# Blockwise causal attention and a gated MLP on one core: Q of the later batches loaded in 2 KB runs, transposed by the crossbar, and read by the score matmuls with a stride

## The chip, the core and the metric

The kernel runs on one core of one Trainium2 chip. The metric is device time in microseconds, the median of several runs. Most executions of one kernel agree within a little over 1%, so differences of a few us are only read from runs of the same rounds, made on the same chip.

## The reference, cut to what matters

```python
# q, k, v: [8 batches, 8 heads, 576 tokens, 64], float32
scores = q @ k.T / 8                         # per batch and head
scores = where(query_token // 64 >= key_token // 64, scores, -1e9)
attn   = softmax(scores)                     # rows
x      = (attn @ v), heads side by side      # [4608, 512]
h      = x @ w_in                            # [512, 2048]
g      = h * sigmoid(beta * h)
out    = g @ w_out                           # [4608, 512], float32
```

## The kernel before

A small planner takes operations with estimated durations, priorities and buffers, simulates them, and writes from that a fixed order of instructions for each engine. The engines then run their orders with semaphore waits only. So an estimate given to the planner changes nothing in an instruction, but it changes the order.

Work goes by head pairs: four per batch, 32 in all. For each pair, K and Q must lie transposed ([128 = 2 heads x 64, tokens]), bfloat16. In batches 0 and 1 TensorE transposes them. In batches 2 to 7 they are loaded as rows of tokens, cast by GpSimd (POOL) and transposed by the DMA crossbar. Both loads of a pair share these parts:

```python
# batches 2..7, every second pair: one load for two pairs, five DMAs, runs of 64 floats = 256 bytes
z = [g.dma_start(ST[ts.slot][:, i, :, :], src[b, h, 128*i:128*i+128, :].rearrange("h p d -> p h d"))
     for i in range(4)]
z.append(g.dma_start(ST[ts.slot][0:64, 4, :, :], src[b, h, 512:576, :].rearrange("h p d -> p h d")))
ld[nm, u] = ld[nm, u + 1] = P.op("SP", 5 * 400, fl, deps=szero, tiles=[ts], xfer=3200, prio=u, ...)
# cast on POOL
o = P.op("POOL", 740, fn, deps=[ld[nm, u]], tiles=[ts, tn], prio=u)
# crossbar transpose, issued from SP: [128 tokens x 5, 128] -> [128, 640]; 1000 and 1500 are planner estimates
g.dma_start_transpose(dst[td.slot][:].rearrange("c (t n) -> c t n", n=128), nat[tn.slot][:, 0:640])
cps[nm] = P.op("SP", 1000, ft, deps=[o], tiles=[td, tn], xfer=1500, prio=-1, ...)
...
# scores^T of a pair: K is stationary, Q streams; the two heads use rows 0-63 and 64-127 of the array
for t, q0, q1, off in blocks:
    for h in range(2):
        r = slice(64 * h, 64 * h + 64)
        z = g.matmul(o, KT[tk.slot][r, 128*t:128*t+m], QT[tq.slot][r, q0:q1])
...
# after attention: TensorE transposes the output, VectorE copies it to xT
return g.tensor_copy(xT[:, c, S*b:S*(b+1)], PSb[:, px.slot, 0:576])
```

The blocks of a pair are 512, 448, 64, 64, 320 and 192 query columns. Two groups of instructions recur in the trace: "x8" (512 + 448 + 64 + 64 columns, two heads each) and "x4" (320 + 192). ACT exponentiates the scores, POOL zeroes the masked parts of E, and TensorE multiplies by V. The MLP then works on chunks of 512 tokens (64 matmuls by `w_in`, 64 by `w_out`), and it fills TensorE between the pairs. All loads, transposes and stores are issued from one in-order queue, SP.

The softmax here doesn't subtract the row's maximum and nothing guards it: scores larger than these inputs give would overflow.

Of the kernel before, what the change touches and what calls it, by code (L numbers as in the profile page):

```python
# [7 lines left out]
bf16 = mybir.dt.bfloat16  # L8
# [262 lines left out]
def bass_blockwise_causal_attn__then__act_swish_beta_kernel(  # L271
# [10 lines left out]
    with es:  # L282
        def sb(name, shape, dt):
            return es.enter_context(nc.sbuf_tensor(name, shape, dt))

        NQ = 2
        NE = 3
        NS = 5
        ST = [sb(f"ST{i}", [128, 5, 4, 64], f32) for i in range(NS)]
        ST6 = [s[0:96].rearrange("p t h d -> p (t h d)")[:, 0:768].rearrange("p (h j d) -> p h j d", h=2, j=6)  # L290
               for s in ST]
        Vs = [sb(f"Vs{i}", [128, 5, 8, 64], f32) for i in range(NQ)]
        Qn = [sb(f"Qn{i}", [128, 768], bf16) for i in range(NQ)]
        Kn = [sb(f"Kn{i}", [128, 768], bf16) for i in range(NQ)]
        Vn = [sb(f"Vn{i}", [128, 5, 8, 66], bf16) for i in range(NQ)]
        QT = [sb(f"QT{i}", [128, 640], bf16) for i in range(3)]
        KT = [sb(f"KT{i}", [128, 640], bf16) for i in range(3)]
# [18 lines left out]
        P = Plan()  # L316
# [18 lines left out]
        def mk(fn):  # L335
            return lambda g, e: fn(g)
# [10 lines left out]
        ones, vzero = [], []  # L347
        for i in range(NQ):
            o = P.op("DVE", 300, mk(lambda g, i=i: g.memset(Vs[i][:, 4, :, :], 0.0)), prio=-8)
            vzero.append(o)  # L350
            o = P.op("POOL", 200, mk(lambda g, i=i: g.memset(Vn[i][:, 4, :, 64:66], 0.0)), prio=-5)
            ones.append(o)
            ones.append(P.op("POOL", 200, mk(lambda g, i=i: g.memset(Vn[i][:, 0:4, :, 64:65], 1.0)), prio=-5))
            for h in range(2):
# [7 lines left out]
                  xfer=100, dma=("d_beta", 1), prio=0.1)  # L362
# [3 lines left out]
                  deps=[bt, c2], tiles=[tb], lat=400, mode="full", prio=5)  # L366
# [3 lines left out]
        szero = [P.op("DVE", 350, mk(lambda g, i=i: g.memset(ST[i][64:128, 4, :, :], 0.0)), prio=-7)  # L370
                 for i in range(NS)]


        win, wout = [], []
        for a in range(4):
# [11 lines left out]
        load, ld = {}, {}  # L387
        tl = {}
        for b in range(B):
            ts, t = P.tile("Vs"), P.tile("V")  # L390
            tl[b] = t
            for h0, h1 in ([(0, 2), (2, 8)] if b == 0 else [(0, 8)]):
                def fv(g, e, ts=ts, b=b, h0=h0, h1=h1):
                    z = []
                    for i in range(4):
                        z.append(g.dma_start(  # L396
                            Vs[ts.slot][:, i, h0:h1, :],
                            v[b, h0:h1, 128 * i:128 * i + 128, :].rearrange("h p d -> p h d")))
                    for o in range(2):
                        z.append(g.dma_start(  # L400
                            Vs[ts.slot][64 * o:64 * o + 64, 4, h0 + o:h1:2, :],
                            v[b, h0 + o:h1:2, 512:576, :].rearrange("h p d -> p h d")))
                    return z

                n = (h1 - h0) / 8
                o = ld["V", b, h0] = P.op("SP", 6 * 400, fv, deps=vzero, tiles=[ts], xfer=5000 * n,
                         prio=(0.5 if h0 == 0 else 2.5) if b == 0 else 4 * b + 0.5 - 3 * (b > 1), dma=["d_V", h0, 6])

                def fw(g, e, ts=ts, t=t, h0=h0, h1=h1):
                    return g.tensor_copy(Vn[t.slot][:, :, h0:h1, 0:64], Vs[ts.slot][:, :, h0:h1, :])  # L410

                o = P.op("POOL", 300 + 2140 * n, fw, deps=[o, *ones], tiles=[ts, t],
                         prio=4 * b + (0.5 if h0 == 0 else 1))
                for h in range(h0, h1, 2):
                    load[4 * b + h // 2] = o
# [4 lines left out]
        for u in range(NU):  # L420
            b, c = divmod(u, NPAIR)
            Tv = tl[b]
            tq, tk = P.tile("QT"), P.tile("KT")
            cps = {}
            for nm, td, src, nat, dst in (("Q", tq, q, Qn, QT), ("K", tk, k, Kn, KT)):
                tn = P.tile(nm)
                if b < 2:

                    ts, pt = P.tile("ST"), P.tile("P1")

                    def fl(g, e, ts=ts, src=src, b=b, c=c):
                        return [g.dma_start(ST6[ts.slot].rearrange("p h j d -> p h (j d)"),
                                            src[b, 2 * c:2 * c + 2].rearrange("h (p j) d -> p h (j d)", j=6))]

                    o = ld[nm, u] = P.op("SP", 420, fl, tiles=[ts], xfer=1050, prio=u, dma=["d_S", 0, 1])

                    def fn(g, e, ts=ts, tn=tn, nat=nat):
                        return g.tensor_copy(nat[tn.slot][0:96, :].rearrange("p (j h d) -> p j h d", j=6, h=2),
                                             ST6[ts.slot].rearrange("p h j d -> p j h d"))

                    o = P.op("DVE", 470, fn, deps=[o], tiles=[ts, tn], prio=-1)

                    def ft(g, e, tn=tn, pt=pt, nat=nat):
                        for i in range(6):
                            z = g.transpose(PSb[:, pt.slot, 96 * i:96 * i + 96],
                                            nat[tn.slot][0:96, 128 * i:128 * i + 128], identB[0:96, 0:96])
                        return z

                    o = P.op("PE", 6 * 57, ft, deps=[o, c4], tiles=[tn, pt, td], lat=6 * 57 + 170, mode="full",
                             prio=pr(u))  # L450

                    def fc(g, e, pt=pt, td=td, dst=dst):
                        return g.tensor_copy(dst[td.slot][:, 0:576].rearrange("c (p j) -> c p j", j=6),
                                             PSb[:, pt.slot, 0:576].rearrange("c (j p) -> c p j", j=6))

                    cps[nm] = P.op("DVE", dve_t(576), fc, deps=[o], tiles=[pt, td], prio=0)
                    continue

                if c % 2 == 0:
                    ts = stage[nm] = P.tile("ST")  # L460

                    def fl(g, e, ts=ts, src=src, b=b, c=c):
                        h = slice(2 * c, 2 * c + 4)
                        z = [g.dma_start(ST[ts.slot][:, i, :, :],  # L464
                                         src[b, h, 128 * i:128 * i + 128, :].rearrange("h p d -> p h d"))
                             for i in range(4)]
                        z.append(g.dma_start(ST[ts.slot][0:64, 4, :, :],
                                             src[b, h, 512:576, :].rearrange("h p d -> p h d")))
                        return z

                    ld[nm, u] = ld[nm, u + 1] = P.op("SP", 5 * 400, fl, deps=szero, tiles=[ts], xfer=3200, prio=u,
                                                     dma=["d_S5", 0, 5])
                ts = stage[nm]

                def fn(g, e, ts=ts, tn=tn, nat=nat, c=c):
                    a = 2 * (c % 2)
                    return g.tensor_copy(nat[tn.slot][:, 0:640].rearrange("p (t h d) -> p t h d", t=5, h=2),  # L477
                                         ST[ts.slot][:, :, a:a + 2, :])

                o = P.op("POOL", 740, fn, deps=[ld[nm, u]], tiles=[ts, tn], prio=u)  # L480

                def ft(g, e, tn=tn, td=td, nat=nat, dst=dst):
                    return [g.dma_start_transpose(dst[td.slot][:].rearrange("c (t n) -> c t n", n=128),
                                                  nat[tn.slot][:, 0:640])]

                cps[nm] = P.op("SP", 1000, ft, deps=[o], tiles=[td, tn], xfer=1500, prio=-1, dma=["d_T" + nm, 0, 1])
            te = P.tile("E")
            ex = []
            zs = []
            for g0 in range(4):  # L490
                ps = P.tile("PP" if g0 < 3 else "P1")

                def fq(g, e, ps=ps, g0=g0, tq=tq, tk=tk):
                    blocks = {0: [(0, 0, 512, 0)], 1: [(1, 128, 576, 0), (0, 512, 576, 448)],
                              2: [(2, 256, 576, 0), (3, 384, 576, 320)], 3: [(4, 512, 576, 0)]}[g0]
                    for t, q0, q1, off in blocks:
                        m = min(128, 576 - 128 * t)
                        for h in range(2):
                            r = slice(64 * h, 64 * h + 64)
                            if g0 < 3:  # L500
                                o = PS[0:m, ps.slot + h, off:off + q1 - q0]
                            else:
                                o = PS[r, ps.slot, 0:64]
                            z = g.matmul(o, KT[tk.slot][r, 128 * t:128 * t + m], QT[tq.slot][r, q0:q1])  # L504
                    return z

                o = P.op("PE", 220 if g0 < 3 else 60, fq, deps=[cps["Q"], cps["K"]], tiles=[ps, tq, tk, te],
# [209 lines left out]
```

## Time and profile before

| | before |
|---|---|
| time, median of 3 | 389.35 us (388.67 to 390.41) |
| span of the profiled run | 389.1 us |
| TensorE busy / not busy | 349.6 / 39.5 us |
| SP's DMA packets | 135,744 |

These are lines of the page: engine busy times, then, in 40 slices of the span, the granted TensorE clock and the DMA busy share in tenths.

```profile
PE 349.6 (90%) x2709; PEld 176.3 (45%) x2753; DVE 168.4 (43%) x347; ACT 209.4 (54%) x306; POOL 96.6 (25%) x204
...
PEclk9985779999999569999999999999999999999999
DMA  7989979897998799698967798413001102002002
```

The reader should see the two dents in the clock row. The first, after slice 3, is the start-up. The second, in slices 14 and 15 (about 126 to 146 us), belongs to the stall that the prediction dissects.

### The profile page before, as it was taken

The numbers are of one execution on the slowest core, as the hardware profiler recorded it, in microseconds if no ns is written. First come the engines' busy times: TensorE is split into PE (matmuls) and PEld (weight loads), VectorE is DVE, ScalarE is ACT, GpSimd is POOL, SyncE is SP. The second block draws the span as 40 slices with busy tenths as digits, with TensorE's granted clock in tenths as the row PEclk, the third lists the DMA queues.
The fourth block names the chain that finished last, engine by engine and source line by source line (L and its number), as shares of the span: only waits on it lengthen the run. The fifth ranks groups of instructions, "written<-read, shape, count | busy, mean of one in ns | idle before, by whom it ended". The sixth has DMA issues, their size and how long they took to land.

```text
span 389.1 us, 6936 instructions
## 1 busy us (share of the span) xinstructions
PE 349.6 (90%) x2709; PEld 176.3 (45%) x2753; DVE 168.4 (43%) x347; ACT 209.4 (54%) x306; POOL 96.6 (25%) x204
## 2 busy tenths in 40 slices
PE   3875969999895789999999999999999999999986
PEld 1552435444452445445545555454554444444432
DVE  5753585217520437413752266512670460550710
ACT  3641648127813458456883788817861551751721
POOL 4390263432202522244153353401100000000000
PEclk9985779999999569999999999999999999999999
DMA  7989979897998799698967798413001102002002
GB/s 173 194 113 229 225 123 180 182 211 168 240 199 176 186 178 199 135 184 205 189 144 167 185 170 144 91 54 89 2 1 56 54 1 83 27 0 83 27 27 81
DMA packets 140384, 50.27 MB, mean 129 GB/s; under 512 B 128560, under 2 KB 135744, under 8 KB 140352
## 3 DMA queue, kind: packets, MB, share of 16 engines
q1 hardware_dynamic: 135744, 45.64, 54.1%
q0 software_dynamic: 4608, 4.20, 7.3%
q8 instruction: 21, 0.34, 0.4%
q14 instruction: 11, 0.09, 0.1%
HBM read 36.71 MB, written 9.44 MB: 119 GB/s over the span
## 4 chain that ended last, share of the span: by engine, by line
PE 68%; DMA 8%; SPq 8%; ACT 7%; DVE 6%; issue 2%; POOL 0%
PE PS L603 29%; PE PS L627 28%; PE PS L546 5%; ACT E L511 5%; PE PS L504 4%; SPq L396 3%; DMA ST<-in_q_dram 3%; ACT th L611 2%; DVE gT L615 2%; DMA KT<-Kn 2%; PE PS L573 2%; SPq L464 2%; DMA w_in<-in_moe_w_in_dram 1%; SPq L400 1%; DMA out_dram<-ost 1%
## 5 line engine op out<-in xcount | busy, mean ns | idle before, releaser
L603 PE MATMUL PS<-xT,w_in 128*128 128x512 bf16 x550 | 135.3, 394 | 6.6 <-DVE xT L579 2.7
L615 DVE SCALAR_TENSOR_TENSOR gT<-th,PS 128x512 bf16<-128x512 f32 x144 | 97.5, 685 | 91.2 <-ACT th L611 91.0
L627 PE MATMUL PS<-w_out,gT 128*128 128x512 bf16 x558 | 125.1, 379 | 4.4 <-DVE gT L615 2.2
L611 ACT ACTIVATE th<-PS,beta 128x512 f32<-128x512 f32 x144 | 98.0, 698 | 42.3 <-PE PS L603 41.1
L511 ACT ACTIVATE E<-PS 128x1024 bf16<-128x1024 f32 x96 | 94.6, 1035 | 40.1 <-PE PS L504 39.9
L627 PEld LDWEIGHTS PS<-w_out,gT 128*128 128x128 bf16 x576 | 54.9, 98 | 68.4 <-DVE gT L615 3.4
L603 PEld LDWEIGHTS PS<-xT,w_in 128*128 128x128 bf16 x576 | 54.0, 101 | 68.9 <-issue 7.8
L638 ACT ACTIVATE ost<-PS 128x512 f32<-128x512 f32 x33 | 19.7, 597 | 94.0 <-PE PS L627 92.2
L504 PE MATMUL PS<-QT,KT 64*128 64x448 bf16 (+5 forms) x384 | 40.9, 303 | 6.6 <-ACT E L511 3.1
L546 PE MATMUL PS<-Vn,E 128*128 128x65 bf16 x960 | 38.0, 201 | 5.5 <-POOL E L519 3.5
L546 PEld LDWEIGHTS PS<-Vn,E 128*128 128x128 bf16 x960 | 35.3, 102 | 12.7 <-POOL E L519 6.6
L579 DVE COPY xT<-PS 128x576 bf16<-128x576 bf16 x32 | 14.5, 454 | 44.1 <-PE PS L573 44.1
L556 DVE RECIPROCAL inv<-PS 128x5 f32<-128x5 f32 x64 | 8.3, 173 | 55.5 <-PE PS L546 55.1
L517 POOL MEMSET E<- 64x128 bf16 x64 | 13.6, 212 | 64.8 <-ACT E L511 60.7
L504 PEld LDWEIGHTS PS<-QT,KT 64*128 64x128 bf16 (+1 forms) x384 | 14.8, 99 | 31.4 <-issue 10.5
L564 DVE TENSOR_TENSOR xq<-PS,inv 128x320 bf16<-128x320 f32 x64 | 28.5, 486 | 0.0
L410 POOL CAST Vn<-Vs 128x2560 bf16<-128x2560 f32 (+2 forms) x9 | 18.8, 2085 | 24.0 <-DMA Vs<-in_v_dram 22.1
L477 POOL CAST Qn<-ST 128x640 bf16<-128x640 f32 x24 | 17.3, 722 | 29.4 <-DMA QT<-Qn 26.7
L477 POOL CAST Kn<-ST 128x640 bf16<-128x640 f32 x24 | 17.3, 723 | 22.0 <-DMA KT<-Kn 19.4
L519 POOL MEMSET E<- 64x256 bf16 x32 | 10.1, 316 | 43.0 <-ACT E L511 42.5
L573 PE MATMUL PS<-identB,xq 128*128 128x128 bf16 (+1 forms) x160 | 17.5, 224 | 1.5 <-DVE xq L564 1.4
L573 PEld LDWEIGHTS PS<-identB,xq 128*128 128x128 bf16 (+1 forms) x160 | 12.5, 100 | 11.8 <-DVE xq L564 2.1
(31 smaller groups left out, 71.3 us busy)
## 6 DMA issues: line engine op xcount, KB each, us to landing
out_dram<-ost SPq DMA_DIRECT2D x36, 256.0 KB, 2.3
Vs<-in_v_dram SPq DMA_DIRECT2D x28, 256.0 KB, 4.6
ST<-in_q_dram SPq DMA_DIRECT2D x48, 128.0 KB, 2.8
ST<-in_k_dram SPq DMA_DIRECT2D x48, 128.0 KB, 2.7
ST<-in_q_dram SPq DMA_DIRECT2D x8, 288.0 KB, 4.2
ST<-in_k_dram SPq DMA_DIRECT2D x8, 288.0 KB, 4.4
w_in<-in_moe_w_in_dram POOLq DMA_DIRECT2D x16, 128.0 KB, 5.7
w_out<-in_moe_w_out_dram POOLq DMA_DIRECT2D x16, 128.0 KB, 4.3
```

Source lines behind the costliest of these rows:

```text
L410: return g.tensor_copy(Vn[t.slot][:, :, h0:h1, 0:64], Vs[ts.slot][:, :, h0:h1, :])
L477: return g.tensor_copy(nat[tn.slot][:, 0:640].rearrange("p (t h d) -> p t h d", t=5, h=2), ST[ts.slot][:, :, a:a + 2, :])
L504: z = g.matmul(o, KT[tk.slot][r, 128 * t:128 * t + m], QT[tq.slot][r, q0:q1])
L511: return g.activation(E3[te.slot][:, g0, :, :], PS[:, ps.slot:ps.slot + 2, :], ACT.Exp, scale=0.125)
L546: z = g.matmul(o, eblk(te, t, i, h), Vn[Tv.slot][:, t, 2 * c + h, 0:65], start=(t == 0), stop=(t == i))
L564: return g.tensor_tensor(xq[tx.slot][:, :, 64 * w:64 * w + 64], a, x, ALU.mult)
L573: z = g.transpose(PSb[:, px.slot, 128 * i:128 * i + r], xq[tx.slot][0:r, i, :], identB[0:r, 0:r])
L603: z = g.matmul(PS[:, ph.slot, :], w_in[:, c, 128 * j:128 * j + 128], xT[:, c, row:row + RC], start=(c == 0), stop=(c == 3))
L611: return g.activation(th[tt.slot][:], PS[:, ph.slot, :], ACT.Tanh, scale=beta[:, j:j + 1])
L615: return g.scalar_tensor_tensor(out=gT[tg.slot][:, j, :], in0=th[tt.slot][:], scalar=1.0, in1=PS[:, ph.slot, :], op0=ALU.add, op1=ALU.mult)
L627: z = g.matmul(PS[:, po.slot, :], gT[tg.slot][:, j, 128 * w:128 * w + 128], w_out[:, j, :], start=(j == 0), stop=(j == NJ - 1))
L638: return g.activation(ost[to.slot][:], PS[:, po.slot, :], ACT.Copy, scale=0.5)
```

## The change

The intent: fewer, longer DMA packets and fewer issues for Q, to relieve SP and the DMA engines. Each partition takes 8 consecutive tokens of two heads, so that a run is 8 x 64 floats = 2 KB. After the cast (72 partitions x 1024) the crossbar gives `QT[c, j*80 + p]` for token `8p + j`. The score matmuls then take the tokens in order by stepping 80 elements (160 bytes) between neighbours. K can't be treated alike without also permuting V. At the same time, estimates of the planner are replaced by values meant to be closer to the measured ones: V issue and transfer, K issue, transpose issue and transfer. In the planner a transfer lands 0.7 us + its entered time + 1.5 us after its issue begins, and the entered times of all DMAs are booked one after another.

```diff
--- before.py
+++ after.py
@@ -289,8 +289,10 @@
         ST = [sb(f"ST{i}", [128, 5, 4, 64], f32) for i in range(NS)]
         ST6 = [s[0:96].rearrange("p t h d -> p (t h d)")[:, 0:768].rearrange("p (h j d) -> p h j d", h=2, j=6)
                for s in ST]
+        ST8 = [s[0:72].rearrange("p t h d -> p (t h d)")[:, 0:1024].rearrange("p (h j d) -> p h j d", h=2, j=8)
+               for s in ST]
         Vs = [sb(f"Vs{i}", [128, 5, 8, 64], f32) for i in range(NQ)]
-        Qn = [sb(f"Qn{i}", [128, 768], bf16) for i in range(NQ)]
+        Qn = [sb(f"Qn{i}", [96, 1024], bf16) for i in range(NQ)]
         Kn = [sb(f"Kn{i}", [128, 768], bf16) for i in range(NQ)]
         Vn = [sb(f"Vn{i}", [128, 5, 8, 66], bf16) for i in range(NQ)]
         QT = [sb(f"QT{i}", [128, 640], bf16) for i in range(3)]
@@ -370,6 +372,8 @@
         szero = [P.op("DVE", 350, mk(lambda g, i=i: g.memset(ST[i][64:128, 4, :, :], 0.0)), prio=-7)
                  for i in range(NS)]
 
+        nzero = [P.op("DVE", 350, mk(lambda g, t=t: g.memset(t[64:96, 768:1024], 0.0)), prio=-7) for t in Qn]
+
 
         win, wout = [], []
         for a in range(4):
@@ -403,7 +407,7 @@
                     return z
 
                 n = (h1 - h0) / 8
-                o = ld["V", b, h0] = P.op("SP", 6 * 400, fv, deps=vzero, tiles=[ts], xfer=5000 * n,
+                o = ld["V", b, h0] = P.op("SP", 3000 + 2200 * n, fv, deps=vzero, tiles=[ts], xfer=6300 * n,
                          prio=(0.5 if h0 == 0 else 2.5) if b == 0 else 4 * b + 0.5 - 3 * (b > 1), dma=["d_V", h0, 6])
 
                 def fw(g, e, ts=ts, t=t, h0=h0, h1=h1):
@@ -435,7 +439,7 @@
                     o = ld[nm, u] = P.op("SP", 420, fl, tiles=[ts], xfer=1050, prio=u, dma=["d_S", 0, 1])
 
                     def fn(g, e, ts=ts, tn=tn, nat=nat):
-                        return g.tensor_copy(nat[tn.slot][0:96, :].rearrange("p (j h d) -> p j h d", j=6, h=2),
+                        return g.tensor_copy(nat[tn.slot][0:96, 0:768].rearrange("p (j h d) -> p j h d", j=6, h=2),
                                              ST6[ts.slot].rearrange("p h j d -> p j h d"))
 
                     o = P.op("DVE", 470, fn, deps=[o], tiles=[ts, tn], prio=-1)
@@ -454,6 +458,28 @@
                                              PSb[:, pt.slot, 0:576].rearrange("c (j p) -> c p j", j=6))
 
                     cps[nm] = P.op("DVE", dve_t(576), fc, deps=[o], tiles=[pt, td], prio=0)
+                    continue
+                if nm == "Q":
+
+                    ts = P.tile("ST")
+
+                    def fl(g, e, ts=ts, src=src, b=b, c=c):
+                        return [g.dma_start(ST8[ts.slot].rearrange("p h j d -> p h (j d)"),
+                                            src[b, 2 * c:2 * c + 2].rearrange("h (p j) d -> p h (j d)", j=8))]
+
+                    o = ld[nm, u] = P.op("SP", 420, fl, tiles=[ts], xfer=1000, prio=u, dma=["d_S", 0, 1])
+
+                    def fn(g, e, ts=ts, tn=tn, nat=nat):
+                        return g.tensor_copy(nat[tn.slot][0:72, :].rearrange("p (j h d) -> p j h d", j=8, h=2),
+                                             ST8[ts.slot].rearrange("p h j d -> p j h d"))
+
+                    o = P.op("POOL", 1080, fn, deps=[o, *nzero], tiles=[ts, tn], prio=u)
+
+                    def ft(g, e, tn=tn, td=td, nat=nat, dst=dst):
+                        return [g.dma_start_transpose(dst[td.slot][:].rearrange("c (j p) -> c j p", j=8),
+                                                      nat[tn.slot][0:80, :])]
+
+                    cps[nm] = P.op("SP", 1280, ft, deps=[o], tiles=[td, tn], xfer=800, prio=-1, dma=["d_T" + nm, 0, 1])
                     continue
 
                 if c % 2 == 0:
@@ -468,7 +494,7 @@
                                              src[b, h, 512:576, :].rearrange("h p d -> p h d")))
                         return z
 
-                    ld[nm, u] = ld[nm, u + 1] = P.op("SP", 5 * 400, fl, deps=szero, tiles=[ts], xfer=3200, prio=u,
+                    ld[nm, u] = ld[nm, u + 1] = P.op("SP", 5 * 570, fl, deps=szero, tiles=[ts], xfer=3200, prio=u,
                                                      dma=["d_S5", 0, 5])
                 ts = stage[nm]
 
@@ -483,14 +509,19 @@
                     return [g.dma_start_transpose(dst[td.slot][:].rearrange("c (t n) -> c t n", n=128),
                                                   nat[tn.slot][:, 0:640])]
 
-                cps[nm] = P.op("SP", 1000, ft, deps=[o], tiles=[td, tn], xfer=1500, prio=-1, dma=["d_T" + nm, 0, 1])
+                cps[nm] = P.op("SP", 1280, ft, deps=[o], tiles=[td, tn], xfer=800, prio=-1, dma=["d_T" + nm, 0, 1])
+
+            def qtok(t, r, a, z, b=b):
+                x = t[r, :]
+                return x[:, a:z] if b < 2 else x.rearrange("c (j p) -> c p j", j=8)[:, a // 8:z // 8, :]
+
             te = P.tile("E")
             ex = []
             zs = []
             for g0 in range(4):
                 ps = P.tile("PP" if g0 < 3 else "P1")
 
-                def fq(g, e, ps=ps, g0=g0, tq=tq, tk=tk):
+                def fq(g, e, ps=ps, g0=g0, tq=tq, tk=tk, qtok=qtok):
                     blocks = {0: [(0, 0, 512, 0)], 1: [(1, 128, 576, 0), (0, 512, 576, 448)],
                               2: [(2, 256, 576, 0), (3, 384, 576, 320)], 3: [(4, 512, 576, 0)]}[g0]
                     for t, q0, q1, off in blocks:
@@ -501,7 +532,7 @@
                                 o = PS[0:m, ps.slot + h, off:off + q1 - q0]
                             else:
                                 o = PS[r, ps.slot, 0:64]
-                            z = g.matmul(o, KT[tk.slot][r, 128 * t:128 * t + m], QT[tq.slot][r, q0:q1])
+                            z = g.matmul(o, KT[tk.slot][r, 128 * t:128 * t + m], qtok(QT[tq.slot], r, q0, q1))
                     return z
 
                 o = P.op("PE", 220 if g0 < 3 else 60, fq, deps=[cps["Q"], cps["K"]], tiles=[ps, tq, tk, te],
```

## The prediction

> **What bounds the kernel now.** I read the page's slices first, then stretches of them, then the two stalled engines in order of time. TensorE is busy 90% of the span, 349.6 of 389.1 us, so I first ask where the other 39.5 us lie. The rows by stretch (us; busy time and instructions of PE, PEld, DVE, ACT, POOL; then granted clock, DMA share, GB/s):
>
> ```profile
> 100.00:120.00 20.00, 18.82 (x149) 9.29 (x148) 4.64 (x13) 6.85 (x11) 1.94 (x6) 1.00 1.01 204
> 120.00:137.70 17.70, 9.67 (x108) 5.86 (x109) 4.37 (x12) 8.91 (x12) 8.06 (x15) 0.64 0.76 175
> 137.70:180.00 42.30, 40.79 (x351) 21.51 (x356) 17.70 (x40) 25.45 (x38) 13.83 (x25) 0.95 0.92 177
> 180.00:240.00 60.00, 58.01 (x587) 30.93 (x596) 30.54 (x71) 45.96 (x68) 22.98 (x47) 1.00 0.90 174
> 240.00:303.00 63.00, 61.52 (x489) 31.16 (x496) 25.53 (x56) 35.32 (x54) 8.18 (x22) 1.00 0.21 54
> ```
>
> There are three stages. Up to 85 us (the first two batches and the weights) TensorE starts up and waits; the change leaves those loads alone. Between 120 and 137.7 us it stalls: 8.0 us idle, and it runs at a granted clock of 0.64. From 137.7 us on it is 97% busy until the end, while the DMA engines are 90% busy to 240 us. In this last stage only TensorE's own work counts: a transfer made cheaper there buys nothing, and anything added to TensorE is paid in full.
>
> The stall is explained by the SP queue in order of time (start, us, then the issue), beside TensorE:
>
> ```profile
> 93.18 2.62 SPq L483 DMA_TRANSPOSE KT<-Kn  x2
> 95.83 1.90 SPq L644 DMA_DIRECT2D out_dram<-ost  x3
> 97.78 2.28 SPq L464 DMA_DIRECT2D ST<-in_k_dram  x4
> ...
> 100.79 3.64 SPq L396 DMA_DIRECT2D Vs<-in_v_dram  x4
> ...
> 106.31 2.83 SPq L464 DMA_DIRECT2D ST<-in_q_dram  x4
> ...
> 109.84 3.35 SPq L396 DMA_DIRECT2D Vs<-in_v_dram  x4
> ...
> 116.30 2.22 SPq L464 DMA_DIRECT2D ST<-in_k_dram  x4
> ...
> 119.24 1.29 SPq L483 DMA_TRANSPOSE KT<-Kn  x1
> ```
> ```profile
> 112.94 7.08 PE L627 MATMUL PS<-w_out,gT 128*128 128x512 bf16 x31
> 122.02 0.76 PE L504 MATMUL PS<-QT,KT 64*128 64x512 bf16 x8 [2.00 <-DMA KT<-Kn]
> ```
>
> The K transposes of the first two head pairs of batch 2 are out at 95.8 us. The third pair's waits behind loads for later pairs and goes out at 119.24 us. TensorE has by then used up all its MLP work (the next row chunk needs batch 2 whole) and waits for exactly that transpose. It is thus the in-order SP queue that bounds this stage.
>
> **What the Trainium skill says.** (1) "SBUF — State Buffer", section "Door 1: The DMA port swizzle", says that SBUF has 16-byte lines, that full bandwidth needs at least two hits per line, and that the free stride ends at 8 bf16. The new score matmuls step 80 bf16 (160 bytes) between neighbouring columns, so every column is on another line. The page gives no size of the penalty, and no TensorE operand of before strides, so this trace can't confirm it. (2) "TensorE: Matmul & The Clock Gate", section "What's actually happening", says that an idle window of about 3.4 us halves the clock; the 0.64 in the stall agrees. (3) "DMA: Bandwidth & Descriptors", section "Why small descriptors are slow (HBM only)", puts a fixed overhead on each packet. The trace agrees: from 180 to 240 us a 0.90 share moves 174 GB/s, or 12.1 GB/s per busy engine, almost all in 256-byte runs, while the tail's 2 KB stores move 40 GB/s at a share of 0.11 (22.7 GB/s). (4) The same page, "Why a DMA increments its semaphore by 16 and not by 1", says that the engine count must divide the outer dimension: 72 partitions give 12 engines instead of 16. No run yet shows that.
>
> **The change part by part.**
>
> Q loads. Batches 2 to 7 had 12 loads of five DMAs (256-byte runs). One such load costs SP 2.25 + 0.61 + gaps, about 2.9 us (the rows at 97.78 us and its neighbours), in all 35 us. Now there are 24 DMAs like those of the first batches, about 0.5 us each: 12 us. SP is spared 23 us. The packets go from 27,648 of 256 bytes to 3,456 of 2 KB: 27,648 x 21 ns less 3,456 x 90 ns (both from the rates above) is 270 engine-us, about 17 us of all 16 engines. That is DMA time off the path except through landings.
>
> The cast on POOL. These rows give its slope (line, operation, form, count | busy, mean ns | idle):
>
> ```profile
> L477 POOL CAST Qn<-ST 128x640 bf16<-128x640 f32 x24 | 17.3, 722 | 29.4 <-DMA QT<-Qn 26.7 <-DMA ST<-in_q_dram 0.9 <-POOL E L517 0.5
> L410 POOL CAST Vn<-Vs 128x2560 bf16<-128x2560 f32 x7 | 16.3, 2322 | 20.6 <-DMA Vs<-in_v_dram 18.7 <-PE PS L546 1.6
> ```
>
> (2322 - 722) / 1920 = 0.83 ns per element, so 1024 columns take about 1.04 us instead of 0.72: 24 x 0.32 = 7.7 us more on an engine that is 25% busy. It costs only where a cast stands ahead of a zeroing of E; under 1 us in sum.
>
> The transposes. 80 x 1024 and 128 x 640 are both 640 packets of 256 bytes; I keep the 1.28 us of SP time and 2.9 us landing.
>
> The order. The planner's costs also change (V, K and transpose issues are now entered at about what SP takes), so every queue is re-ordered. In the built program, between the last transpose of the second pair and the K transpose of the third there stand three stores, three single Q DMAs, two K loads, one V load and one Q transpose: 1.5 + 1.6 + 5.8 + 5.4 + 1.3 = 15.6 us, plus two K transposes of 1.3 us, against 24.7 us before (95.8 to 120.5). The block before it also shrinks, but one store now stands in it and makes SP wait for the first output tile (about 5 us, by my walk through TensorE's order). By that walk the third pair's K lands at about 111 us instead of 122, and the next MLP chunk starts near 127.5 us instead of 137.7. The gain is about 10 us: most of the 8.0 us idle, and most of the clock loss (9.67 us of work at 0.64 costs some 3.5 us), less a remainder, since two pairs still depend on their exponentials with no MLP work between.
>
> The score matmuls. Per pair and head they stream 512 + 448 + 64 + 64 + 320 + 192 = 1600 columns, the two heads side by side in different rows. These rows show that the contiguous form runs close to a column per cycle (x8 is 1088 columns and starts 0.70 us before the next group):
>
> ```profile
> 163.63 0.77 PE L504 MATMUL PS<-QT,KT 64*128 64x512 bf16 x8
> 164.33 3.63 PE L627 MATMUL PS<-w_out,gT 128*128 128x512 bf16 x16
> ```
>
> At 2.4 columns per ns, 1600 columns are 0.67 us. If one column per line halves the rate (my reading of "two hits", an estimate), each of the 24 pairs costs 0.67 us more: 16 us. The five pairs before the next MLP chunk take 3.3 us of it, of which I let 1 us vanish in waits; the other 19 take 12.7 us on a TensorE that is 97% busy. Sum: -10 + 2.3 + 12.7 = +5 us, 394 us.
>
> **The rivals.**
>
> A. The stride is free: then only the stall's gain is left, 389.35 - 10 = 379 us, faster by 2.6%. For it: VectorE's copy out of PSUM with steps of 192 bytes takes 750 ns for 576 elements, which is an element per cycle with no further penalty; and the author left the planner's time for the score matmuls as it was. Against: TensorE asks for a column every 0.42 ns, over twice as often as that copy, and the skill's warning names this case.
>
> B. The stride costs much more than half (a line per ns or worse, perhaps the two heads in turn): +32 us or so on TensorE, 405 to 415 us. Nothing in the trace speaks for it; I keep one chance in ten.
>
> C. The stall doesn't go: the store ahead of the second Q load, or the five ST buffers (a Q pair now takes one for itself, where two pairs shared one) holds loads back as long as the five DMAs did. Then the gain is 3 us or less, and with the half rate the time is about 402 us. For it: SP is in order, and the stores wait for ACT. Against: the stretch between the transposes is shorter by count.
>
> **How range and chances follow.** I give half rate 0.6, free 0.3, worse 0.1. Half rate spreads from 388 (the gain is larger, or some cost hides) to 402 (rival C); free from 377 to 385. The point is set a little under the half-rate sum, for rival A's weight: 392 us. The range for eight in ten runs from 379.5 to 401. Faster by over 2% (under 381.6) needs a free stride and the whole gain: 0.24. Slower by over 2% (over 397.1) comes from rivals B and C: 0.26. Within 2%: 0.5.
>
> **What would show it.** The strided score groups between MLP groups: an x8 group near 0.70 us says free, near 1.15 us says half rate. The stretch from 120 to 138 us: a clock near 1.00 and under 4 us idle says that the stall is gone; a wait on the K transpose there says rival C. Q packets down by 24,192, the DMA share from 140 to 240 us well under 0.9, the Q cast at 1.04 us. If TensorE's busy time is about 16 us up and the time still falls, the stall was worth more than I took it for; if it is unchanged and the time doesn't fall, the order is at fault and not the stride.

## More of the kernel before

The causal mask works on blocks of 64 tokens. The order of tokens *inside* such a block is free as long as it is put right before the output; one experiment uses this.

The widest score matmuls in the list of groups (count | busy, mean ns | idle time before them and what ended it), and an x4 group in order of time with the group after it (start, us, then the group):

```profile
L504 PE MATMUL PS<-QT,KT 64*128 64x512 bf16 x64 | 13.6, 418 | 3.2 <-DMA KT<-Kn 2.0 <-DVE KT L453 1.0
...
145.08 0.41 PE L504 MATMUL PS<-QT,KT 64*128 64x320 bf16 x4
145.42 4.49 PE L603 MATMUL PS<-xT,w_in 128*128 128x512 bf16 x20
```

The trace of before lacks some matmul records (2709 of 2753), so its TensorE busy time is slightly understated.

## The result, and the profile after

The changed kernel takes 431.97 us (431.47 to 432.62, 3 runs): slower by 10.9%, ratio 1.1092 with a 95% interval of 1.1046 to 1.1139. The prediction was 392 us with a range of 379.5 to 401: wrong, and wrong by much.

The same lines of the page after (line numbers of the source have moved by some 30 lines):

```profile
PE 407.0 (94%) x2753; PEld 174.5 (41%) x2753; DVE 167.9 (39%) x346; ACT 219.5 (51%) x309; POOL 104.3 (24%) x204
...
PEclk9977969999995999999999998999999999999999
DMA  7799998999999954978859323202100200201101
```

TensorE's busy time rose by 57.4 us (407.0 - 349.6) and its idle time fell by 15.7 us (39.5 to 23.8); 57.4 - 15.7 = 41.7 us is the growth of the span (430.8 - 389.1). From 140 us to the end of the slices TensorE has no idle to speak of. These are rows by stretch (us; busy time and instructions of PE, PEld, DVE, ACT, POOL; clock, DMA share, GB/s) of the changed kernel:

```profile
120.00:140.00 20.00, 18.98 (x125) 7.43 (x124) 3.84 (x11) 9.13 (x13) 7.54 (x12) 0.74 1.14 237
140.00:160.00 20.00, 20.00 (x113) 6.96 (x111) 10.05 (x18) 15.45 (x22) 4.92 (x10) 1.00 0.89 148
160.00:180.00 20.00, 20.00 (x196) 8.62 (x195) 7.22 (x22) 10.09 (x14) 9.39 (x15) 1.00 0.74 137
180.00:200.00 20.00, 20.00 (x146) 8.26 (x144) 3.15 (x10) 8.86 (x13) 5.74 (x12) 1.00 0.80 174
```

The idle time at 120 us is gone (the clock there is still 0.74), but TensorE is busy with something longer. What that is shows in the order of time on TensorE (start, us, then the group):

```profile
99.20 1.15 PE L535 MATMUL PS<-QT,KT 64*128 64x320 bf16 x4
100.28 3.63 PE L634 MATMUL PS<-xT,w_in 128*128 128x512 bf16 x16
...
114.31 2.37 PE L535 MATMUL PS<-QT,KT 64*128 64x512 bf16 x8
116.61 0.60 PE L658 MATMUL PS<-w_out,gT 128*128 128x512 bf16 x2
```

From start to the next group's start, an x8 group takes 2.30 us (0.70 before) and an x4 group 1.08 us (0.34 before; the recorded expectations of e1 and e6 put it lower, 0.22 us in e1). That is 2.1 ns for each of the 1600 columns of a pair. Per pair it is 3.38 instead of 1.04 us, and 24 x 2.34 = 56 us in all. The MLP groups beside them are unchanged. The groups of before that were shown above, and the cast, after:

```profile
L535 PE MATMUL PS<-QT,KT 64*128 64x512 bf16 x64 | 31.7, 983 | 0.9 <-DVE KT L457 0.9
...
L473 POOL CAST Qn<-ST 72x1024 bf16<-72x1024 f32 x24 | 24.9, 1037 | 19.4 <-DMA QT<-Qn 11.7 <-DMA ST<-in_q_dram 6.2
```

The mean of 983 ns still mixes 16 contiguous matmuls of the first two batches into the 64. The cast is where it was predicted (1.04 us).

### The profile page after: what moved, and what is told of

It reads as the page before. It is cut to its first block, busy times and chain, and to the rows that moved or that the text cites. A ratio compares the mean times of both kernels' runs of the same rounds, so it can differ in the third digit from the quotient of the medians.

```text
span 430.8 us, 6947 instructions
## 1 busy us (share of the span) xinstructions
PE 407.0 (94%) x2753; PEld 174.5 (41%) x2753; DVE 167.9 (39%) x346; ACT 219.5 (51%) x309; POOL 104.3 (24%) x204
## 4 chain that ended last, share of the span: by engine, by line
PE 69%; ACT 0%; DVE 0%; issue 0%
PE PS L634 24%; PE PS L658 23%; PE PS L535 15%; PE PS L577 5%; PE PS L604 2%; DVE gT L646 0%; ACT th L642 0%; ACT ost L669 0%
## 5 line engine op out<-in xcount | busy, mean ns | idle before, releaser
L634 PE MATMUL PS<-xT,w_in 128*128 128x512 bf16 x576 | 140.0, 395 | 0.9 <-DVE xT L610 0.6
L658 PE MATMUL PS<-w_out,gT 128*128 128x512 bf16 x576 | 127.9, 380 | 1.5 <-DVE gT L646 1.5
L542 ACT ACTIVATE E<-PS 128x1024 bf16<-128x1024 f32 x96 | 96.7, 1026 | 62.3 <-PE PS L535 62.3
L535 PE MATMUL PS<-QT,KT 64*128 64x448 bf16 (+5 forms) x384 | 96.6, 599 | 2.5 <-ACT E L542 1.7
L669 ACT ACTIVATE ost<-PS 128x512 f32<-128x512 f32 x36 | 21.5, 597 | 103.9 <-PE PS L658 103.9
L577 PE MATMUL PS<-Vn,E 128*128 128x65 bf16 x960 | 36.5, 199 | 4.6 <-POOL E L550 3.9
L535 PEld LDWEIGHTS PS<-QT,KT 64*128 64x128 bf16 (+1 forms) x384 | 15.9, 102 | 60.2 <-issue 40.4
L577 PEld LDWEIGHTS PS<-Vn,E 128*128 128x128 bf16 x960 | 34.1, 101 | 14.3 <-POOL E L550 3.1
L473 POOL CAST Qn<-ST 72x1024 bf16<-72x1024 f32 x24 | 24.9, 1037 | 19.4 <-DMA QT<-Qn 11.7
```

Source lines behind the costliest of these rows:

```text
L473: return g.tensor_copy(nat[tn.slot][0:72, :].rearrange("p (j h d) -> p j h d", j=8, h=2), ST8[ts.slot].rearrange("p h j d -> p j h d"))
L535: z = g.matmul(o, KT[tk.slot][r, 128 * t:128 * t + m], qtok(QT[tq.slot], r, q0, q1))
L542: return g.activation(E3[te.slot][:, g0, :, :], PS[:, ps.slot:ps.slot + 2, :], ACT.Exp, scale=0.125)
L577: z = g.matmul(o, eblk(te, t, i, h), Vn[Tv.slot][:, t, 2 * c + h, 0:65], start=(t == 0), stop=(t == i))
L634: z = g.matmul(PS[:, ph.slot, :], w_in[:, c, 128 * j:128 * j + 128], xT[:, c, row:row + RC], start=(c == 0), stop=(c == 3))
L658: z = g.matmul(PS[:, po.slot, :], gT[tg.slot][:, j, 128 * w:128 * w + 128], w_out[:, j, :], start=(j == 0), stop=(j == NJ - 1))
```

## The experiments

Theory 1: the strided read of the moving operand costs one fetch of a 16-byte line for each column, and this is the whole loss. Theory 2: the new order or the Q loads cost much of it. Theory 3: any break of the unit step costs, whatever the lines. Twelve kernels were run. The time of before in the same rounds is given each time.

**e1, the score reads without the stride.** The same loads, buffers and order, but contiguous columns. The tokens are then in a wrong order. The comparison with the reference still passes: at these inputs (q and k are 0.1 times normal random numbers, so scores are about 0.01) attention is nearly uniform, and the check can't see it. So a passed check says nothing about the order of tokens in any of the kernels here.

```diff
-                return x[:, a:z] if b < 2 else x.rearrange("c (j p) -> c p j", j=8)[:, a // 8:z // 8, :]
+                return x[:, a:z]
```

> The changed kernel whose score matmuls read the same bytes of Q without the stride (tokens in a wrong order, so the result is wrong on purpose). Theory 1, the strided read is the whole loss: an x8 group of scores falls from 2.3 to 0.70 us, an x4 group from 1.09 to 0.22 us, 24 x 2.5 = 60 us come off an engine that is 97% busy, and the time is 370 to 376 us, below the kernel before. Theory 2, much of the loss is in the new order of the queues or in the Q loads: the time stays at or above 389 us though the groups are short.

Measured: 399.66 us (before: 389.43), ratio 1.0257 (1.0196 to 1.0318). All score matmuls together take 40.6 us of TensorE, as in before (40.9). So the stride accounts for 432.0 - 399.7 = 32 us of the time, but this is not the whole account: without it the kernel is still 10 us *slower* than before. Theory 1 isn't the whole, and theory 2 has a share. The waits of TensorE from 85 to 260 us in this run (waiter <- what ended it: us in total, times, longest):

```profile
PE PS L535 <- DMA KT<-Kn: 9.1, 5, 3.8
PE PS L577 <- POOL E L550: 4.5, 3, 2.8
PE PS L535 <- DMA QT<-Qn: 2.7, 3, 1.8
```

The matmuls wait for transposes of K and Q, and for POOL's zeroing. From 180 to 220 us TensorE is busy only 31.7 of 40 us, where before it was 39.2.

**e2, runs of 8.** The same loads and order, but the 64 tokens of a block are read as eight runs of 8 neighbours (each 16 bytes, one line), and the copy to `xT` puts the tokens back. That the order is then right follows from the indices (`QT` holds token 8p + j at 80j + p), not from the check.

```diff
-                return x[:, a:z] if b < 2 else x.rearrange("c (j p) -> c p j", j=8)[:, a // 8:z // 8, :]
+                return x[:, a:z] if b < 2 else x.rearrange("c (j g q) -> c g j q", j=8, q=8)[:, a // 64:z // 64, :, :]
...
-                return g.tensor_copy(xT[:, c, S * b:S * (b + 1)], PSb[:, px.slot, 0:576])
+                if b < 2:
+                    return g.tensor_copy(xT[:, c, S * b:S * (b + 1)], PSb[:, px.slot, 0:576])
+                return g.tensor_copy(xT[:, c, S * b:S * (b + 1)].rearrange("c (g q j) -> c g q j", q=8, j=8),
+                                     PSb[:, px.slot, 0:576].rearrange("c (g j q) -> c g q j", j=8, q=8))
-            xt.append(P.op("DVE", 425, fy, deps=[xp], tiles=[px], prio=0))
+            xt.append(P.op("DVE", 425 if b < 2 else dve_t(576), fy, deps=[xp], tiles=[px], prio=0))
```

> The changed kernel with the columns of each group of 64 tokens read as eight runs of 8 neighbours (16 bytes) instead of one by one; the copy to xT puts the tokens back in order, so the result is right. Theory 1 (the cost is one 16-byte line per column): the score groups are back to 0.70 and 0.22 us, the xT copies of batches 2 to 7 go from 0.45 to 0.75 us on an idle VectorE, and the time is within 4 us of the contiguous run, 371 to 378 us. Theory 3 (any break of the unit step, or a third dimension, costs): the groups stay well above 1 us and the time above 395 us.

Measured: 399.57 us (389.43), ratio 1.0276 (1.0206 to 1.0345): the time of e1. The score matmuls take 41.3 us, so the break of the unit step every 8 columns and the third dimension cost nothing that shows. Theory 3 falls. The reordering copies take 0.75 instead of 0.45 us, beside other work. The absolute time was expected at 371 to 378 and missed by 22 us; e1 missed its range by 24 us.

**e3, the planner's new estimates alone.** The kernel before with the new estimates, its own loads and contiguous reads.

```diff
-P.op("SP", 6 * 400, fv, deps=vzero, tiles=[ts], xfer=5000 * n,
+P.op("SP", 3000 + 2200 * n, fv, deps=vzero, tiles=[ts], xfer=6300 * n,
-P.op("SP", 5 * 400, fl, deps=szero
+P.op("SP", 5 * 570, fl, deps=szero
-P.op("SP", 1000, ft, deps=[o], tiles=[td, tn], xfer=1500
+P.op("SP", 1280, ft, deps=[o], tiles=[td, tn], xfer=800
```

> The kernel before with only the planner's four new costs (V issue and transfer, K and Q issue, transpose issue and transfer), Q loaded and read as before. If the order that these costs make is what takes the stall away: 372 to 380 us, the wait on the third pair's K transpose gone. If the cheaper Q loads are what does it: 386 to 392 us, the stall still there.

Measured: 395.7 us (389.43), ratio 1.0157 (1.0105 to 1.021). Neither expectation holds: the new estimates make the old kernel 6 us slower.

**e4, the read by itself.** Not this program (the result is wrong): one line per way of reading, 24 matmuls per head, 512 columns, all operands set in advance to constants, one execution.

```python
J  = X[:, 0:640].rearrange("c (j p) -> c p j", j=8)            # the change's pattern
Gq = X[:, 0:640].rearrange("c (j g q) -> c g j q", j=8, q=q)   # runs of q = 2, 4, 8
for n in range(24):
    for h in (0, 1):                                           # a pair: rows 0-63 and 64-127
        g.matmul(PS[:, 2*(n % 4) + h, :], W[R[h], :], <X, or J, or Gq>[R[h], ...])
```

> Not this program: 24 pairs of 64-row matmuls of 512 columns for each way of reading the moving operand, back to back (wrong result on purpose). Contiguous pairs: about 0.22 us a pair. Theory 1 (lines): steps of 2 and 4 elements cost little, from 8 elements (16 bytes) on about 1.09 us a pair, no more at 16 or 80; runs of 2 about half of that, of 4 a quarter, of 8 contiguous speed. Theory 3 (any stride): step 2 already costs about 1.09 us. Heads in turn: one head alone with the stride takes half of a pair, 0.55 us; heads beside each other: one head alone takes the same 1.09 us.

TensorE in order of time (start, us, line). Line 44 is the warm-up; then pairs: 47 contiguous, 50 step 2, 53 step 4, 56 step 8, 59 step 16, 62 step 80, 65 the change's pattern, 68, 71 and 74 runs of 2, 4 and 8. Then 76 and 78 are one head alone, contiguous and with the change's pattern, and 82 is one matmul of all 128 rows with that pattern.

```profile
50.41 5.34 PE L47 MATMUL PS<-X,W 64*128 64x512 bf16 x48
55.59 5.58 PE L50 MATMUL PS<-X,W 64*128 64x512 bf16 x48
61.01 11.00 PE L53 MATMUL PS<-X,W 64*128 64x512 bf16 x48
71.84 21.77 PE L56 MATMUL PS<-X,W 64*128 64x512 bf16 x48
93.44 22.20 PE L59 MATMUL PS<-X,W 64*128 64x512 bf16 x48
115.46 24.12 PE L62 MATMUL PS<-X,W 64*128 64x512 bf16 x48
139.41 24.02 PE L65 MATMUL PS<-X,W 64*128 64x512 bf16 x48
163.25 12.07 PE L68 MATMUL PS<-X,W 64*128 64x512 bf16 x48
175.14 6.10 PE L71 MATMUL PS<-X,W 64*128 64x512 bf16 x48
181.08 5.34 PE L74 MATMUL PS<-X,W 64*128 64x512 bf16 x48
186.26 5.34 PE L76 MATMUL PS<-X,W 64*128 64x512 bf16 x24
191.44 24.00 PE L78 MATMUL PS<-X,W 64*128 64x512 bf16 x24
...
223.26 24.00 PE L82 MATMUL PS<-X,W 128*128 128x512 bf16 x24
```

Start to start, divided by 24, and by the number of 16-byte lines that 512 columns touch in order:

| read | us per 512 columns | lines touched | ns per line |
|---|---|---|---|
| contiguous | 0.216 | 64 | 3.4 (not the bound) |
| step 2 | 0.226 | 128 | 1.76 |
| step 4 | 0.451 | 256 | 1.76 |
| step 8 | 0.900 | 512 | 1.76 |
| step 16 | 0.918 | 512 | 1.79 |
| step 80 | 0.998 | 512 | 1.95 |
| the change's pattern | 0.993 | 512 | 1.94 |
| runs of 2 | 0.495 | 256 | 1.93 |
| runs of 4 | 0.248 | 128 | 1.93 |
| runs of 8 | 0.216 | 64 | 3.4 (not the bound) |

Nearly one number explains all rows: a line costs 1.76 to 1.95 ns, whatever is taken from it. A contiguous read needs a new line only every 3.4 ns, so it isn't held up. A line must give at least four columns to stay near full speed, not two. I had expected step 4 to be nearly free, and it halves the speed. One head alone takes as long as a pair (0.216 and 1.00 us), and so does the 128-row form with the stride (1.00 us). The heads therefore run beside each other also when strided, and they don't share the rate.

The clock had not been expected. These are rows by stretch of this run for steps 4, 8 and 16:

```profile
61.00:71.80 10.80, 10.80 (x50) 2.72 (x48) 0.00 (x0) 0.00 (x0) 1.00 0.00 0
71.80:93.40 21.60, 21.60 (x50) 2.94 (x48) 0.00 (x0) 0.00 (x0) 0.55 0.00 1
93.40:115.40 22.00, 22.00 (x50) 2.99 (x48) 0.00 (x0) 0.00 (x0) 0.50 0.00 0
```

TensorE never idles, yet the granted clock falls to half (the column before the DMA share). This isn't the cause of the slowness: step 4 pays 1.76 ns per line at a clock of 1.00 and step 8 the same at 0.55, and in the changed kernel the clock is 1.00 from 140 us on while the strided columns take 2.1 ns. Nor does the kernel's 2.1 ns contradict the 1.94 ns here: an x4 group (512 columns) takes about 0.1 us more in the kernel than in this bench in both forms (1.08 against 0.993 us strided, 0.34 against 0.216 us contiguous), and an x8 group about 0.2 us more in both. The columns alone would thus cost 24 x 1600 x (1.94 - 0.42) ns = 58 us.

**e5, runs of 8 with the planner's old estimates.** e2 with e3's edit taken back.

```diff
-P.op("SP", 3000 + 2200 * n, fv, deps=vzero, tiles=[ts], xfer=6300 * n,
+P.op("SP", 6 * 400, fv, deps=vzero, tiles=[ts], xfer=5000 * n,
-P.op("SP", 5 * 570, fl, deps=szero
+P.op("SP", 5 * 400, fl, deps=szero
-P.op("SP", 1280, ft, deps=[o], tiles=[td, tn], xfer=800      # both places, Q and K
+P.op("SP", 1000, ft, deps=[o], tiles=[td, tn], xfer=1500
```

> The kernel of the runs of 8 (right result, score reads at full speed) with the planner's three old costs for V, K and transposes. If the new costs alone make the bad order (as in the costs-only run, +6 us), this is below the kernel before: 380 to 387 us, a version that beats both. If the single Q loads and their ST buffers are what disturbs the order, it stays at 393 to 400 us.

Measured: 384.09 us (391.0), ratio 0.9864 (0.9789 to 0.9939). This beats the kernel before, by 0.6 to 2.1%, and the changed one by far. Against e2 only the estimates differ, and they make 15 us (of other rounds; e11 against e10, in the same rounds, makes 16). Its page and its row over the old stall:

```profile
PE 348.6 (92%) x2753; PEld 172.9 (45%) x2753; DVE 175.4 (46%) x348; ACT 208.8 (55%) x307; POOL 104.0 (27%) x204
```
```profile
120.00:140.00 20.00, 16.96 (x176) 9.02 (x174) 10.16 (x22) 13.73 (x22) 9.82 (x17) 0.91 0.94 211
```

The stall has shrunk from 8.0 us idle at a clock of 0.63 (120 to 140 us of before) to 3.0 us idle at 0.91.

**e6, the stride alone.** The kernel before (loads, order, estimates), with the change's strided view laid over its contiguous Q. Its output is wrong, which doesn't matter for the time. The order of the queues is that of before.

```diff
-z = g.matmul(o, KT[tk.slot][r, 128 * t:128 * t + m], QT[tq.slot][r, q0:q1])
+z = g.matmul(o, KT[tk.slot][r, 128 * t:128 * t + m], qtok(QT[tq.slot], r, q0, q1))   # qtok as in the change
```

> The kernel before (loads, costs and order unchanged) with the score matmuls of batches 2 to 7 reading Q with the stride of 80 (wrong tokens on purpose). Theory 1: 24 pairs of heads x 1600 columns x (2.13 - 0.57 ns, both as measured in the two kernels in place) = 60 us of TensorE time, less what the 8 us stall and smaller waits swallow: 435 to 449 us, the stall at 120 to 138 us shorter. If the stride hurts only together with the new order: under 415 us.

Measured: 436.61 us (391.0), ratio 1.1191 (1.1129 to 1.1254), as theory 1 says. TensorE is busy 408.2 us. The stride by itself makes 45.6 us, more than the whole loss of the change.

**e7, the change with the old estimates.** e5's edit applied to the changed kernel, stride kept.

> The changed kernel, stride and all, with the planner's three old costs. If order and stride simply add: 432 - 6 = 426 us. If TensorE is the bound either way and the order no longer matters under the stride: 429 to 434 us.

Measured: 436.87 us (391.0), ratio 1.1193 (1.1117 to 1.1269).

```profile
PE 408.2 (94%) x2753; PEld 175.1 (40%) x2753; DVE 169.6 (39%) x348; ACT 218.6 (50%) x307; POOL 103.7 (24%) x204
```

It is above both expectations, though above the second by only 3 us, with before 1.6 us slower in these rounds. Against e6 (436.61), only the Q loads and the order that goes with them differ, and they make nothing: under the stride TensorE is the bound from 140 us on, and what comes in sooner just waits. Against e5 the reading differs, and the copy to `xT` with its estimate. Both traces have all 2753 matmul records, so this is the best measure of TensorE's time: TensorE busy 408.2 - 348.6 = 59.6 us more, of which the score matmuls make 57.9 (97.5 - 39.6), and time 436.9 - 384.1 = 52.8 us more. What the stride is worth in time depends on what else waits: 32 us in the new order (the change against e1), 46 in the old one (e6 against before), 53 here. The remaining 7 us went into waits that the longer scores filled.

**e8, a third Qn buffer.** e5 with three Qn buffers instead of two.

```diff
-        Qn = [sb(f"Qn{i}", [96, 1024], bf16) for i in range(NQ)]
+        Qn = [sb(f"Qn{i}", [96, 1024], bf16) for i in range(3)]
-("Q", NQ)
+("Q", 3)
```

> As the runs of 8 with the old costs, and three Qn buffers instead of two, so that a Q cast need not wait for the transpose two pairs earlier. If that wait (POOL in order, with the zeroing of E behind it) is what costs the new layout its time: 3 us or more faster than with two buffers. If it is not: within 2 us.

Measured: 386.43 us (391.0), ratio 0.9904 (0.9855 to 0.9952). It is not faster than e5, whose interval overlaps. POOL's wait for that buffer fell from 26.8 to 6.7 us, and the time didn't follow.

**e9, runs of 2.** e5 with q=2 in place of q=8 (blocks of 16 tokens), order right by the indices. This sets the "two hits per line" of the Trainium skill ("SBUF — State Buffer", section "Door 1: The DMA port swizzle") against e4's line cost, in the kernel.

```diff
-x.rearrange("c (j g q) -> c g j q", j=8, q=8)[:, a // 64:z // 64, :, :]
+x.rearrange("c (j g q) -> c g j q", j=8, q=2)[:, a // 16:z // 16, :, :]
-xT[...].rearrange("c (g q j) -> c g q j", q=8, j=8), PSb[...].rearrange("c (g j q) -> c g q j", j=8, q=8)
+xT[...].rearrange("c (g q j) -> c g q j", q=2, j=8), PSb[...].rearrange("c (g j q) -> c g q j", j=8, q=2)
```

> As the runs of 8 with the old costs (384 us), but columns read as runs of 2 neighbours (4 bytes), eight such runs 160 bytes apart; result right. The skill's figure (two hits per 16-byte line suffice): the same time, 382 to 388 us. The bench (one line per 1.9 ns whatever is taken from it, so 0.495 instead of 0.216 us per 512 columns): 0.87 us more for each of 24 pairs, 21 us on TensorE less some 3 to 8 us swallowed by waits: 397 to 403 us; x8 groups near 1.2 us.

Measured: 395.58 us (389.61), ratio 1.0151 (1.0108 to 1.0194). The score matmuls take 59.2 us against 39.6 in e5: 19.6 us more, where 21 were expected from e4. The time rose by 11.5 us (e5 is of other rounds), a little less than expected. Two hits don't suffice. TensorE in order of time in this run:

```profile
158.14 1.31 PE L535 MATMUL PS<-QT,KT 64*128 64x320 bf16 x8
159.38 3.63 PE L661 MATMUL PS<-w_out,gT 128*128 128x512 bf16 x15
```

1.24 us for x8, against 0.69 for the same group in e5 (at 154.20 us) and 2.33 for such a group with the stride (at 181.94 us in the changed kernel).

**e10, e11, e12: which estimate.** e5 with the new V estimates alone (e10), with the new transpose estimates alone (e11), and with only the first of those two (e12):

```diff
e10: -P.op("SP", 6 * 400, fv, deps=vzero, tiles=[ts], xfer=5000 * n,
     +P.op("SP", 3000 + 2200 * n, fv, deps=vzero, tiles=[ts], xfer=6300 * n,
e11: -P.op("SP", 1000, ft, deps=[o], tiles=[td, tn], xfer=1500
     +P.op("SP", 1280, ft, deps=[o], tiles=[td, tn], xfer=800
e12: -P.op("SP", 1000, ft, deps=[o], tiles=[td, tn], xfer=1500
     +P.op("SP", 1280, ft, deps=[o], tiles=[td, tn], xfer=1500
```

> The runs of 8 with the old costs, except that the planner is given the new cost of V loads. If the V cost is what turns 384 into 399 us: 393 us or more. If it is the transposes' cost: 382 to 389 us.

> The runs of 8 with the old costs, except that the planner is given the new cost of the transposes (SP 1280, transfer 800 instead of 1000 and 1500), by which it believes that transposed K and Q arrive sooner and puts pairs closer together. If that is what makes TensorE wait for K: 393 us or more with waits on the K transpose. If it is the V cost: 382 to 389 us.

> The runs of 8 with the old costs, except that the planner is given 1280 instead of 1000 as SP's time for a transpose; the transfer stays 1500. If the shortened transfer (1500 to 800, pairs planned closer together than the chip delivers) makes the bad order of the 401.7 us run: 381 to 388 us here. If it is the issue time: 395 us or more.

Measured: e10 385.28 us (389.61), ratio 0.9888 (0.9843 to 0.9933). e11 401.67 us (389.61), ratio 1.0307 (1.0255 to 1.036). e12 383.78 us (390.23), ratio 0.9843 (0.9778 to 0.9907); e5 and e12 are the same within their intervals. So of all the new estimates it is the transposes' transfer, 800 instead of 1500 and entered together with the issue of 1280, that costs the 15 us. TensorE's longest waits from 85 to 260 us, first in e5, then in e11:

```profile
PE PS L535 <- ACT E L542: 1.9, 4, 0.8
PE PS L637 <- DVE gT L649: 1.1, 2, 0.7
```
```profile
PE PS L535 <- DMA QT<-Qn: 5.0, 2, 2.6
PE PS L577 <- POOL E L550: 4.7, 4, 2.7
PE PS L535 <- DMA KT<-Kn: 1.7, 2, 1.5
```

With the short estimate TensorE waits for transposes and for POOL; with the long one these waits are gone from the top. POOL's waits for a K transpose to free its buffer grew from 4.5 to 21.8 us, and its zeroings of E stand behind those casts. The likely reading is that the longer estimate acts as slack: it holds a score group further behind its transpose, and the in-order queues of SP and POOL then have room for landings and buffer waits that the planner doesn't foresee. No run shows this reasoning apart from the number itself. A rival stands beside it: since the planner books the transfers of all DMAs one after another, 48 transposes at 800 instead of 1500 ns also take 34 us out of that booking and pull every later load forward in the plan. Nor is the short estimate simply the truer one. It plans a landing 3.0 us after the issue, the long one 3.7 us; measured were 2.7 to 2.9 us (medians) in the kernel before, but 3.4 to 3.5 us in e5.

Put together (us; rows: loads and estimates):

| | full-speed score reads | stride of 80 |
|---|---|---|
| old loads, old estimates | 389.4 to 391.0 (before) | 436.6 (e6) |
| old loads, new estimates | 395.7 (e3) | not run |
| new loads, old estimates | 384.1 (e5) | 436.9 (e7) |
| new loads, new estimates | 399.6 (e2), 399.7 (e1) | 432.0 (the change) |

Without the stride the new estimates hurt, by 15 us with the new loads and 6 with the old. Under it they don't (432.0 against 436.9 us, but of different rounds and with intervals that overlap, so that a gain is not shown). An order is good or bad for the durations that it meets.

## Why the prediction was wrong, point by point

**The score matmuls: the step that failed.** The prediction priced the stride at half rate, "16 us". It measured 57.9 us in the score matmuls (59.6 us in all of TensorE, e7 against e5), because a column on a line of its own costs 1.94 ns (e4), 2.1 ns with all that a group takes, and not 0.83 ns (two columns' time). The mechanism named was right: the cost is by 16-byte lines (e2, e4, e9). The term was mis-sized by 3.6, for I turned "at least two hits per line" into a rate. Rival B named the right direction ("a line per ns or worse"), but its size of "+32 us or so" was too small as well, and it got one chance in ten. My evidence for rival A, VectorE's copy with far steps in 750 ns, came from PSUM and another engine. It says nothing about TensorE's read of SBUF, and it wasn't free either: the contiguous copy of the same size (to `xT`) takes 454 ns in the same trace. Another reading was loose: x8 starts 0.70 us before the next group for 1088 columns, 1.55 columns per ns and not 2.4. The sum used only the columns' own rate, so little hung on it.

**The stall.** The idle time did go, as predicted: in the changed kernel the stretch from 120 to 140 us is 19.0 of 20 us busy. The clock did not come back: it was 0.74 there, where the prediction had named "near 1.00" as the sign, and the 12 matmuls by `w_in` at 136.33 us took 4.39 us, 0.37 us each against 0.22 elsewhere. This fits e4, where strided reads went with a lower clock; no run separates it. That the idle time went gained nothing, as e7 against e6 shows, for the strided scores fill the stretch with their own length even with the old loads (16.5 of 20 us busy in e6). With full-speed reads the loads and a suitable order gain 5 to 7 us (e5, e12), where the prediction had 10.

**The order.** The prediction walked the new order to the next MLP chunk and put the third pair's K at 111 us and the chunk at 127.5. In e1, the same order without the stride, the K arrives with the scores at 112.3 us, but the chunk starts at 133.0. Between the two, TensorE's order has the scores of the fifth pair ahead of the fourth's last transposes: the fifth's K transpose stands behind a V load that holds SP from 118.6 to 125.4 us, goes out at 126.8, and TensorE waits 3.8 us for it. After that comes what the walk had left out: the order goes on to 300 us. From 180 to 220 us TensorE idled 8.3 us in e1, against 0.8 before. The assumption that the re-ordering helps everywhere because it helps at the known stall failed: e3 is 6 us slower by the estimates alone, and e11 names the one. Rival C looked for the loss in the first store and the ST buffers; by e1's waits and e11 it lay with the transposes of later pairs.

**The smaller terms.** The cast took 1.04 us as computed. A Q transpose of 80 x 1024 takes SP 1.28 us and lands in 2.9 us, as assumed. Packets on SP's queue fell by 24,864: the 24,192 data packets of the prediction, and 672 more, which is 60 DMAs x 16 less 24 x 12 completion packets. So Q's DMAs do run on 12 engines. The "17 us of all 16 engines" did not appear: the summed packet time of SP's queue went from 3268 (47.1% of 433.6 us x 16, e6) to 3342 engine-us (48.2% of 433.3 us x 16, e7), up by 2%. The median landing of K's loads beside the Q loads rose from 2.7 to 3.9 us (2.8 in e6, 3.4 in e7). So the time per packet, taken from one stretch, didn't carry over; whether it contains waiting was not shown. Whether the 2 KB packets or the 12 engines delay the neighbours was not separated.

**The chances.** About 1 in 10 was given to anything over 401 us, and even rival B ended at 415. What makes this wrong beyond bad luck is that the sum rested on a factor that neither the skill nor the trace gave, and the range was drawn around that factor.

## What to carry to other kernels

A moving operand of a matmul should take four or more neighbours (8 bytes of bfloat16; 15% over contiguous in e4), better the whole 16-byte line (nothing over), before it jumps. Where a layout forces a stride, permute within a block that the rest of the kernel treats as a unit, read whole lines, and undo the order in a copy on an engine with time to spare. When estimates feed a scheduler, test each alone on the chip: one meant to be truer can give a worse order, and an order tuned for one duration of TensorE's work isn't tuned for another. A cost without a measured size is measured by itself first, or the range is made to hold all of its plausible sizes.

## What the Trainium skill lacked or had wrong

- "SBUF — State Buffer", section "Door 1: The DMA port swizzle": full bandwidth from two hits per 16-byte line does not hold for TensorE's moving operand. Two hits give 0.495 us per 512 columns and four give 0.248 us against 0.216 us contiguous. The page gives no size for the penalty; here a line costs 1.76 ns (even steps of up to 16 bytes) to 1.95 ns.
- The same section puts the free step at up to 8 bf16 elements. Here step 2 costs 5% (0.226 us), step 4 halves the rate (0.451 us), and step 8 is a quarter of it (0.900 us).
- "TensorE: Matmul & The Clock Gate", section "What's actually happening": the clock follows how busy TensorE is. It does not say how a TensorE counts that is held up by its operand: in the e4 run the granted clock was 0.50 to 0.55 in the stretches of steps 8 and 16, where the profile shows TensorE busy throughout, and 1.00 at step 4, which runs at half rate. Why is open.
- "DMA: Bandwidth & Descriptors", section "Why small descriptors are slow (HBM only)": the fixed overhead on each packet that it names did not turn into a saving here: with 24,192 fewer data packets, on 12 engines instead of 16, the summed packet time stayed (3268 to 3342 engine-us). This is no refutation, since packets and engines changed together. The page gives no figure for what long packets do to the short ones beside them; K's median landing rose from 2.8 to 3.4 us (e6, e7).
